# Token groups across sequences, chunk 0 on the hardware queues, three-chunk first MLP blocks, and stores issued by ScalarE

## Chip, cores and metric

The kernel runs on one core of one Trainium2 chip. The metric is device microseconds (us) by the run's timer. The trace of a run gives a *span*, from its first to its last instruction; on this kernel the timer reads about 1.8 us more than the span of the same run (219.26 against 217.5 for the trace of the kernel before).

Names: PE is TensorE, ACT is ScalarE, DVE is VectorE, POOL is GpSimd, SP is SyncE. A `q` behind a name (ACTq, SPq) marks the engine's sequencer issuing a transfer. Of the tiles, `q_hat` and `k_dec` are q and k multiplied by powers of the decay, and `qT` and `kT` are the transposed tiles.

## The reference, cut to what matters

```python
# q, k, v: (4 sequences, 8 heads, 768 tokens, 64); lam: one decay per head; blocks of 64 tokens
for b in range(nb):
    intra = (qb @ kb^T * Dmask) @ vb
    inter = (qb * lam_pow) @ kv_state
    out[:, :, sl] = intra + inter
    kv_state = lam_block * kv_state + (kb * rev_pow)^T @ vb      # serial along one sequence
x = out.transpose(0, 2, 1, 3).reshape(4 * 768, 512)
h = x @ w_in                                                      # 512 -> 2048
y = gelu_exact(h) @ w_out                                         # 2048 -> 512, float32 out
```

The kernels work in chunks of 128 tokens: 24 chunks, six in each sequence. The state is serial along a sequence and independent between sequences. Four chunks make a *group* of 512 tokens, and the MLP runs group by group, six groups in all. The attention of the next group is woven between the MLP's matmuls.

## The kernel before: the parts that matter here

A group is four successive chunks, whichever sequence they belong to (`b, so = n // 6, n % 6`). All casting loads are on POOL, all stores on SP.

```python
qkv_pool = tile_pool("qkv", bufs=8);  work_pool = tile_pool("work", bufs=3)
out_pool = tile_pool("outp", bufs=3)
# ... cut
nc.sync.dma_start(lam_b, lam[None, :].to_broadcast((128, H)))
nc.gpsimd.iota(pos, ...);  nc.gpsimd.iota(row, ...)
for item in "k0 q0 v0 k1 q1 k2 q2 v1 k3 q3 v2 v3".split():
    load(int(item[1]), item[0])                  # nc.gpsimd.dma_start, float32 -> bf16
# ... later: load_w_in(0), the first quarter of w_in, is POOL's 13th transfer

def dma_transposes(c):                           # chunks 8 to 23: transposed by the DMA engines
    nc.sync.dma_start_transpose(out=c.kT, in_=c.k...)
    nc.gpsimd.tensor_mul(q_hat, c.q, lam_p...)
    nc.sync.dma_start_transpose(out=c.qT, in_=q_hat...)

def mm2(io, part):                               # second MLP product of one chunk, in four parts
    # ... cut: four matmuls per part
    if part == NK2 // 4 - 1:
        o_sb = out_pool.tile([128, d_model], F32, tag="o_s", name="o_sb")
        nc.scalar.copy(o_sb, om[io])
        nc.sync.dma_start(out[r:r + C, :], o_sb) # the store
# ... cut: chunks 0 to 3 before the MLP; chunks 8 to 23 one by one, at set shares of a group
```

Of the kernel before, what the change touches and what calls it, by code (L numbers as in the profile page):

```python
# [8 lines left out]
F32 = mybir.dt.float32  # L9
# [6 lines left out]
def kernel(  # L16
# [23 lines left out]
    M = 4  # L40
    NG = NCH // M
    assert NG * M == NCH and M == 4 and NB == 6

# [4 lines left out]
    qkv_pool = ctx.enter_context(tc.tile_pool(name="qkv", bufs=8))  # L48
    work_pool = ctx.enter_context(tc.tile_pool(name="work", bufs=3))
# [9 lines left out]
    def chunk_of(name, n):  # L59
        b, so = n // NB, n % NB  # L60
        return dram[name][b, :, so * C:(so + 1) * C, :].rearrange("h si d -> si h d")
# [4 lines left out]


    lam_b = consts.tile([128, H], F32)
    nc.sync.dma_start(lam_b, lam[None, :].to_broadcast((128, H)))

    pos = consts.tile([128, 1], F32)
# [3 lines left out]

    for item in "k0 q0 v0 k1 q1 k2 q2 v1 k3 q3 v2 v3".split():
        load(int(item[1]), item[0])
# [14 lines left out]

    idle = consts.tile([128, 512], BF16)
# [4 lines left out]
    cmj = consts.tile([128, 1], F32)  # L98
    warm = consts.tile([128, 1], F32)
    nc.vector.tensor_scalar(ident, row, pos, None, op0=ALU.is_equal)  # L100
    nc.vector.tensor_scalar(cmask, row, pos, None, op0=ALU.is_ge)
    nc.vector.tensor_scalar(negj, pos, -1.0, None, op0=ALU.mult)
    nc.vector.tensor_scalar(cmj, pos, -1.0, float(C), op0=ALU.mult, op1=ALU.add)

    lam_blk = consts.tile([128, HP, 128], F32)
    first_blk = consts.tile([128, HP, 128], BF16)
    nc.vector.memset(lam_blk, 0.0)
    nc.vector.memset(first_blk, 0.0)
# [7 lines left out]
    lam_k = consts.tile([128, H], F32)  # L116
# [10 lines left out]
    nc.scalar.activation(lam_k, ln, ACT.Exp, scale=cmj)  # L127
    nc.scalar.activation(lam_c, ln_col, ACT.Exp, scale=float(C))
    nc.scalar.activation(lam_p, ln, ACT.Exp, scale=pos)
    lam_c_b = lam_c[:, :, None].to_broadcast((128, HP, D))  # L130

    def make_lam_blk():
        for hi in range(2):
            p = slice(hi * D, (hi + 1) * D)
            nc.vector.tensor_copy(lam_blk[p, :, p], lam_c_b[p])
# [10 lines left out]
    states = {}  # L146

    def bank(shape, dtype, tag, name):
        return ps.tile(shape, dtype, tag=tag, name=name, bufs=2 if tag in ("sc", "mh", "mo") else 1)

    def begin(n, early=False):
        c = Chunk()
        c.n, c.sb, c.early = n, n % NB, early
        c.q, c.k, c.v = (raw.pop((n, name)) for name in "qkv")
        return c

    def decay_k(c, eng):

        if c.sb == NB - 1:
            return  # L160
        c.k_dec = work_pool.tile([128, H, D], BF16, tag="kd", name="k_dec")
        if eng is nc.scalar:
            for h in range(H):
                nc.scalar.activation(c.k_dec[:, h, :], c.k[:, h, :], ACT.Copy, scale=lam_k[:, h:h + 1])
        else:
            scale = lam_k if c.early else lam_m
            eng.tensor_mul(c.k_dec, c.k, scale[:, :, None].to_broadcast((128, H, D)))  # L167

    def transposes(c, between=lambda: None):

        t_ps = [bank([128, HP, C], BF16, tag, "t_ps") for tag in ("mh", "mo" if c.early else "mh")]
# [7 lines left out]
        if c.n > 0:  # L179
            nc.scalar.copy(c.kT, t_ps[0])  # L180
        else:
            nc.vector.tensor_copy(c.kT, t_ps[0])
# [21 lines left out]
    def next_state(c):  # L204
        if c.sb == NB - 1:
            return
        if not c.early:
            return next_state_full(c)
        kv_ps = bank([128, HP, D], F32, "t", "kv_ps")
        for hp in range(HP):  # L210
            for hi in range(2):
                h = 2 * hp + hi
                nc.tensor.matmul(kv_ps[hi * D:(hi + 1) * D, hp, :], c.k_dec[:, h, :], c.v[:, h, :],
                                 start=True, stop=True)
        if c.n == M - 1:
            for hi in range(2):
                p = slice(hi * D, (hi + 1) * D)
                nc.vector.tensor_add(first_blk[p, :, p], kv_ps[p], states[c.n][1][p])
            states[c.n + 1] = first_blk, None
            return  # L220
        new = work_pool.tile([128, HP, D], BF16, tag="state", name="state")
        if c.sb == 0:
            nc.vector.tensor_copy(new, kv_ps)
        else:
            nc.vector.tensor_add(new, kv_ps, states[c.n][1])
        old = work_pool.tile([128, HP, D], F32, tag="old", name="old")
        states[c.n + 1] = new, old

    def decay_state(c):
        new, old = states[c.n + 1]  # L230
        for hp in range(HP):
            nc.scalar.activation(old[:, hp, :], new[:, hp, :], ACT.Copy, scale=lam_c[:, hp:hp + 1])

    def next_state_full(c):

        kv_ps = bank([128, HP, 128], F32, "t", "kv_ps")
# [3 lines left out]
        new = work_pool.tile([128, HP, 128], BF16, tag="state_f", name="state")  # L240
        if c.sb == 0:
            nc.vector.tensor_mul(new, kv_ps, lam_blk)
        else:
            tmp = work_pool.tile([128, HP, 128], F32, tag="tmp", name="tmp")
            nc.vector.tensor_add(tmp, kv_ps, states[c.n][0])  # L245
            nc.vector.tensor_mul(new, tmp, lam_blk)  # L246
        states[c.n + 1] = new, None

    def outputs(c, x_t, off, evacuate=True):
        o_ps = bank([128, HP, C], F32, "o", "o_ps")  # L250
        if c.sb > 0 and not c.early:
            for hp in range(HP):
                nc.tensor.matmul(o_ps[:, hp, :], states[c.n][0][:, hp, :], c.qT[:, hp, :],  # L253
                                 start=(hp == 0), stop=False, skip_group_check=True)
        elif c.sb > 0:
            for hp in range(HP):
                for hi in range(2):
                    p = slice(hi * D, (hi + 1) * D)
                    nc.tensor.matmul(o_ps[p, hp, :], states[c.n][0][p, hp, :], c.qT[p, hp, :],
                                     start=(hp == 0), stop=False, skip_group_check=True)  # L260
        for hp in range(HP):
            for hi in range(2):
                nc.tensor.matmul(o_ps[hi * D:(hi + 1) * D, hp, :], c.v[:, 2 * hp + hi, :], c.sc_m[:, hp, hi, :],  # L263
                                 start=(c.sb == 0 and hp == 0), stop=True, skip_group_check=True)
        c.x_o, c.o_ps = x_t[:, :, off * C:(off + 1) * C], o_ps
        if evacuate:
            empty_outputs(c)

    def empty_outputs(c):
        if c.n < 2 * M:  # L270
            nc.scalar.copy(c.x_o, c.o_ps)
        else:
            nc.vector.tensor_copy(c.x_o, c.o_ps)  # L273


    def mlp_blocks(g):
        T = M * C
        x_t = xT[g]
        g_t = g_pool.tile([128, NK2, T], BF16, tag="g", name="g_t")

        def mm1(kf):
            def run():
                h_ps = bank([128, T], F32, "mh", "h_ps")

                parts = [(0, T - C), (T - C, T)] if g == 0 and kf == 0 else [(0, T)]
                for lo, hi in parts:
                    for ki in range(NK1):
                        nc.tensor.matmul(h_ps[:, lo:hi], w_in_t[:, ki, kf * 128:(kf + 1) * 128], x_t[:, ki, lo:hi],  # L288
                                         start=(ki == 0 and lo == 0), stop=(ki == NK1 - 1), skip_group_check=True)
                nc.scalar.activation(g_t[:, kf, :], h_ps, ACT.Gelu)  # L290
            return run
# [3 lines left out]
        def mm2(io, part):  # L295
            def run():
                if part == 0:
                    om[io] = bank([128, d_model], F32, "mo", "o2_ps")
# [3 lines left out]
                if part == NK2 // 4 - 1:  # L302
                    o_sb = out_pool.tile([128, d_model], F32, tag="o_s", name="o_sb")
                    r = (g * M + io) * C
                    nc.scalar.copy(o_sb, om[io])  # L305
                    nc.sync.dma_start(out[r:r + C, :], o_sb)
            return run

        def mm2_half(io, half):

            def run():
                w = slice(half * (d_model // 2), (half + 1) * (d_model // 2))
                o2 = bank([128, d_model // 2], F32, "mo", "o2_ps")
# [4 lines left out]
                r = (g * M + io) * C  # L318
# [5 lines left out]
        blocks = [(mm1(kf), 4 * T) for kf in range(NK2)]  # L324
# [15 lines left out]
    next_load = [M]  # L340
# [6 lines left out]


    alloc_x(0)
    live = {}  # L350
    make_dmask()
    nc.scalar.activation(warm, pos, ACT.Gelu)

    idle_ps = {}

    def keep_warm(n, new=True):

        if new:
            idle_ps[0] = bank([128, 512], F32, "mo", "idle_ps")
        for _ in range(n):  # L360
            nc.tensor.matmul(idle_ps[0], idle[:, :128], idle, start=True, stop=True)  # L361

    def early(s, between=lambda: None):
        live[s] = begin(s, early=True)
        if s == 1:
            decay_k(live[s], nc.vector)
        transposes(live[s], between)
        if s != 1:
            decay_k(live[s], nc.scalar if s == 0 else nc.gpsimd)

    keep_warm(9)
    early(0, lambda: keep_warm(3, new=False))
    keep_warm(2, new=False)
    scores(live[0])
    keep_warm(2, new=False)
    early(1)
# [128 lines left out]
```

## Time and profile before

| | us |
|---|---|
| timer, median of 3 runs (lowest to highest) | 217.46 (217.44 to 217.77) |
| timer and span of the traced run | 219.26 and 217.5 |
| busy PE / ACT / POOL in the span | 204.9 / 91.1 / 105.8 |
| first MLP matmul | 19.37 |
| groups 0 to 4, from first matmul to first matmul of the next | 34.68, 35.12, 32.41, 32.19, 32.42 |
| group 5 with the tail | 31.31 |

### The profile page before, as it was taken

The numbers are of one execution on the slowest core, as the hardware profiler recorded it, in microseconds if no ns is written. First come the engines' busy times: TensorE is split into PE (matmuls) and PEld (weight loads), VectorE is DVE, ScalarE is ACT, GpSimd is POOL, SyncE is SP. The second block draws the span as 40 slices with busy tenths as digits, with TensorE's granted clock in tenths as the row PEclk, the third lists the DMA queues.
The fourth block names the chain that finished last, engine by engine and source line by source line (L and its number), as shares of the span: only waits on it lengthen the run. The fifth ranks groups of instructions, "written<-read, shape, count | busy, mean of one in ns | idle before, by whom it ended". The sixth has DMA issues, their size and how long they took to land.

```text
span 217.5 us, 3545 instructions
## 1 busy us (share of the span) xinstructions
PE 204.9 (94%) x1422; PEld 102.9 (47%) x1446; DVE 74.8 (34%) x120; ACT 91.1 (42%) x169; POOL 105.8 (49%) x120
## 2 busy tenths in 40 slices
PE   7679999999987999999999999999999999999993
PEld 2355444555443544444545444544445545444452
DVE  5884000478516243316225323315415323100000
ACT  6975772434563321365221375221465221566121
POOL 8998333998999999276950809113000000000000
PEclk9999999999999999999999999999999999999998
DMA  5999999999999999999999497515251012100112
GB/s 37 149 169 203 198 194 183 156 208 148 177 150 126 164 128 138 215 110 104 109 114 160 77 180 62 37 48 146 74 98 24 3 57 88 50 0 3 48 49 96
DMA packets 100272, 24.35 MB, mean 112 GB/s; under 512 B 92960, under 2 KB 97312, under 8 KB 100256
## 3 DMA queue, kind: packets, MB, share of 16 engines
q0 software_dynamic: 79104, 13.64, 84.4%
q1 hardware_dynamic: 21152, 10.50, 22.7%
q8 instruction: 11, 0.18, 0.3%
q14 instruction: 5, 0.04, 0.1%
HBM read 27.27 MB, written 6.29 MB: 154 GB/s over the span
## 4 chain that ended last, share of the span: by engine, by line
PE 73%; DMA 14%; POOL 9%; issue 2%; ACT 0%; POOLq 0%
PE o_ps L300 33%; PE h_ps L288 28%; DMA q_t<-in_q_dram 8%; DMA qT<-q_hat 3%; DMA w_in_t<-in_moe_w_in_dram 3%; PE o_ps L263 3%; PE sc_ps L198 3%; POOL k_t L65 3%; POOL q_t L65 2%; POOL v_t L65 2%; PE kv_ps L238 2%; PE o_ps L315 2%; PE o_ps L253 2%; POOL k_dec L167 1%; POOL q_hat L190 1%
## 5 line engine op out<-in xcount | busy, mean ns | idle before, releaser
L288 PE MATMUL h_ps<-x_t,w_in_t 128*128 128x512 bf16 (+2 forms) x378 | 84.8, 377 | 1.0 <-DMA w_in_t<-in_moe_w_in_dram 0.5
L300 PE MATMUL o_ps<-w_out_t,g_t 128*128 128x512 bf16 x355 | 81.8, 379 | 0.8 <-issue 0.3
L290 ACT ACTIVATE g_t<-h_ps 128x512 bf16<-128x512 f32 x96 | 57.3, 597 | 35.3 <-PE h_ps L288 35.3
L288 PEld LDWEIGHTS <-w_in_t 128*128 128x128 bf16 x388 | 37.3, 98 | 43.8 <-DMA w_in_t<-in_moe_w_in_dram 0.6
L300 PEld LDWEIGHTS <-g_t 128*128 128x128 bf16 x368 | 34.7, 98 | 39.6
L305 ACT COPY o_sb<-o_ps 128x512 f32<-128x512 f32 x23 | 13.5, 586 | 68.3 <-PE o_ps L300 62.5
L202 DVE TENSOR_TENSOR sc_m<-sc_ps,dmask 128x512 bf16<-128x512 f32 x48 | 30.8, 683 | 16.1 <-PE sc_ps L198 15.8
L273 DVE CAST x_t<-o_ps 128x512 bf16<-128x512 f32 x16 | 11.1, 692 | 71.4 <-PE o_ps L263 71.4
L190 POOL TENSOR_TENSOR q_hat<-q_t,lam_p 128x512 bf16<-128x512 bf16 x16 | 16.9, 1056 | 20.0 <-DMA qT<-q_hat 19.0
L167 POOL TENSOR_TENSOR k_dec<-k_t,lam_m 128x512 bf16<-128x512 bf16 x16 | 17.7, 1106 | 14.0 <-PE kv_ps L238 8.1
L65 POOL DMA_DIRECT2D k_t<-in_k_dram x24 | 22.1, 920 | 4.0 <-DMA w_out_t<-in_moe_w_out_dram 2.1
L65 POOL DMA_DIRECT2D q_t<-in_q_dram x24 | 21.5, 897 | 4.2 <-DMA w_out_t<-in_moe_w_out_dram 3.4
L65 POOL DMA_DIRECT2D v_t<-in_v_dram x24 | 21.4, 894 | 3.4 <-DMA w_out_t<-in_moe_w_out_dram 1.7
L198 PE MATMUL sc_ps<-qT,kT 64*128 64x128 bf16 x192 | 9.5, 218 | 3.8 <-DMA qT<-q_hat 2.6
L246 DVE TENSOR_TENSOR state<-tmp,lam_blk 128x512 bf16<-128x512 f32 x13 | 12.1, 932 | 0.5
L183 DVE TENSOR_TENSOR qT<-t_ps,lam_q 128x512 bf16<-128x512 bf16 x8 | 5.5, 689 | 18.9 <-PE t_ps L174 18.7
L263 PE MATMUL o_ps<-sc_m,v_t 128*64 128x128 bf16 x192 | 10.1, 225 | 0.0
L198 PEld LDWEIGHTS <-kT 64*128 64x128 bf16 x192 | 5.7, 94 | 8.3 <-issue 4.7
L361 PE MATMUL idle_ps<-idle 128*128 128x512 bf16 x21 | 7.5, 473 | 1.2 <-DVE idle L94 1.2
L245 DVE TENSOR_TENSOR tmp<-kv_ps,state 128x512 f32<-128x512 f32 x12 | 8.2, 681 | 0.0
L180 ACT COPY kT<-t_ps 128x512 bf16<-128x512 bf16 x7 | 4.1, 579 | 9.4 <-PE t_ps L174 9.4
L263 PEld LDWEIGHTS <-v_t 128*64 128x64 bf16 x192 | 6.2, 109 | 3.3 <-issue 0.8
(57 smaller groups left out, 82.7 us busy)
## 6 DMA issues: line engine op xcount, KB each, us to landing
out_dram<-o_sb SPq DMA_DIRECT2D x23, 256.0 KB, 2.6
k_t<-in_k_dram POOLq DMA_DIRECT2D x24, 128.0 KB, 4.6
q_t<-in_q_dram POOLq DMA_DIRECT2D x24, 128.0 KB, 5.9
v_t<-in_v_dram POOLq DMA_DIRECT2D x24, 128.0 KB, 5.9
w_in_t<-in_moe_w_in_dram POOLq DMA_DIRECT2D x4, 512.0 KB, 7.9
w_out_t<-in_moe_w_out_dram POOLq DMA_DIRECT2D x4, 512.0 KB, 15.1
kT<-k_t SPq DMA_TRANSPOSE x16, 4.7
qT<-q_hat SPq DMA_TRANSPOSE x16, 4.0
```

Source lines behind the costliest of these rows:

```text
L65: nc.gpsimd.dma_start(raw[n, name], chunk_of(name, n))
L167: eng.tensor_mul(c.k_dec, c.k, scale[:, :, None].to_broadcast((128, H, D)))
L190: nc.gpsimd.tensor_mul(q_hat, c.q, lam_p[:, :, None].to_broadcast((128, H, D)))
L198: nc.tensor.matmul(sc_ps[hi][:, hp, :], c.kT[p, hp, :], c.qT[p, hp, :], start=True, stop=True)
L202: nc.vector.tensor_mul(c.sc_m[:, :, hi, :], sc_ps[hi], dmask_r[:, :, hi, :])
L246: nc.vector.tensor_mul(new, tmp, lam_blk)
L263: nc.tensor.matmul(o_ps[hi * D:(hi + 1) * D, hp, :], c.v[:, 2 * hp + hi, :], c.sc_m[:, hp, hi, :], start=(c.sb == 0 and hp == 0), stop=Tru ...
L273: nc.vector.tensor_copy(c.x_o, c.o_ps)
L288: nc.tensor.matmul(h_ps[:, lo:hi], w_in_t[:, ki, kf * 128:(kf + 1) * 128], x_t[:, ki, lo:hi], start=(ki == 0 and lo == 0), stop=(ki == NK1 ...
L290: nc.scalar.activation(g_t[:, kf, :], h_ps, ACT.Gelu)
L300: nc.tensor.matmul(om[io], g_t[:, kf, io * C:(io + 1) * C], w_out_t[:, kf, :], start=(kf == 0), stop=(kf == NK2 - 1))
L305: nc.scalar.copy(o_sb, om[io])
```

## The change

The intent: start the MLP sooner, by taking chunk 0 off POOL's queue and letting the first MLP blocks run on three chunks; make the four chunks of a group independent (`b, so = n % 4, n // 4`), so that states and scores can be fed in pairs and asked for early; and free SP's queue for transposes, by letting ACT issue the stores.

```diff
-        b, so = n // NB, n % NB
+        b, so = n % B, n // B
-    qkv_pool = ... bufs=8        work_pool = ... bufs=3
+    qkv_pool = ... bufs=12       work_pool = ... bufs=6
     # outp keeps bufs=3
+    k_f = load_f32(0, "k", nc.scalar)
     nc.sync.dma_start(lam_b, lam[None, :].to_broadcast((128, H)))
+    q_f = load_f32(0, "q", nc.sync)
+    v_f = load_f32(0, "v", nc.sync)
+    load(1, "k")
     # ... the two iotas
-    for item in "k0 q0 v0 k1 q1 k2 q2 v1 k3 q3 v2 v3".split():
+    for item in "q1 k2 q2 v1 v2 k3 q3".split():
+    load_w_in(0)
+    load(3, "v")
     # ... cut
-            parts = [(0, T - C), (T - C, T)] if g == 0 and kf == 0 else [(0, T)]
+        split = g < 2            # first four blocks on three chunks, then one block for the fourth
     # ... cut
-                    nc.sync.dma_start(out[r:r + C, :], o_sb)
+                    nc.scalar.dma_start(out[r:r + C, :], o_sb)
     # ... cut
+    round_f32(0, "k", k_f, nc.vector.tensor_copy)
+    round_f32(0, "q", q_f, nc.vector.tensor_copy)
+    nc.scalar.copy(live[0].v, v_f)
+    # chunks 4 to 9 loaded, 8 and 9 requested; then k_dec of 4 to 7 on POOL
+    # groups 1 to 4: pair_a (two scores), pair_b (two inter, two kv, two intra), at set blocks
```

## The prediction

> **What bounds it now.** I read the page's busy table first, then the chain of waits, then the timeline in three stretches (start-up, group 0 to group 1, and the tail).
>
> ```profile
> PE 204.9 (94%) x1422; PEld 102.9 (47%) x1446; DVE 74.8 (34%) x120; ACT 91.1 (42%) x169; POOL 105.8 (49%) x120
> ...
> PE 73%; DMA 14%; POOL 9%; issue 2%; ACT 0%; POOLq 0%
> ```
>
> TensorE (PE) is the bound: nothing else passes 49%, and where the chain is not PE it is the start-up and the loads. So three things are worth time: when the dense MLP stream begins, how much PE work lies after that, and where PE stands still inside it. The timeline of the start-up answers the first:
>
> ```profile
> 11.99 0.84 POOL L87 DMA_DIRECT2D w_in_t<-in_moe_w_in_dram  x1
> ...
> 18.94 0.59 ACT L271 CAST x_t<-o_ps 128x512 bf16<-128x512 f32 x1 [1.50 <-PE o_ps L263]
> 19.37 0.88 PEld L288 LDWEIGHTS <-w_in_t 128*128 128x128 bf16 x8 [0.63 <-DMA w_in_t<-in_moe_w_in_dram]
> 19.37 1.05 PE L288 MATMUL h_ps<-x_t,w_in_t 128*128 128x384 bf16 x8 [0.47 <-DMA w_in_t<-in_moe_w_in_dram]
> ...
> 20.59 13.12 PE L288 MATMUL h_ps<-x_t,w_in_t 128*128 128x512 bf16 x59
> ```
>
> The MLP starts at 19.37 us, when the first quarter of w_in lands, 7.4 us after its issue at 11.99. The fourth chunk's x_t is ready at 19.53, so both limits stand together. From 20.59 to 33.55 lie 60 matmuls of 512 columns (one record is missing), so 0.216 us each. The PE timeline gives the cost of the attention's pieces, as differences of start times:
>
> ```profile
> 41.23 0.40 PE L198 MATMUL sc_ps<-qT,kT 64*128 64x128 bf16 x8
> 41.56 1.04 PE L300 MATMUL o_ps<-w_out_t,g_t 128*128 128x512 bf16 x4
> 42.44 0.39 PE L174 MATMUL t_ps<-ident,k_t 128*128 128x128 bf16 x4
> 42.66 0.39 PE L174 MATMUL t_ps<-ident,q_t 128*128 128x128 bf16 x4
> 42.88 0.39 PE L238 MATMUL kv_ps<-v_t,k_dec 128*128 128x128 bf16 x4
> 43.10 0.39 PE L253 MATMUL o_ps<-qT,first_blk 128*128 128x128 bf16 x4
> 43.42 0.41 PE L263 MATMUL o_ps<-sc_m,v_t 128*64 128x128 bf16 x8
> 43.77 1.04 PE L300 MATMUL o_ps<-w_out_t,g_t 128*128 128x512 bf16 x3
> ...
> 56.32 0.40 PE L198 MATMUL sc_ps<-qT,kT 64*128 64x128 bf16 x8 [0.38 <-DMA qT<-q_hat]
> ...
> 66.70 0.40 PE L198 MATMUL sc_ps<-qT,kT 64*128 64x128 bf16 x8 [2.18 <-DMA qT<-q_hat]
> ```
>
> Scores cost 0.33, transposes 0.44, the state (kv) 0.22, the inter part 0.32, the intra part 0.35. Inter takes as many matmuls as kv, so 0.10 of it is the turn to the narrower 128x64 tile of intra. The last two lines are the only large stalls of PE after the start: 0.4 and 2.2 us for a transposed q. The last matmul run ends at 214.06, and 3.4 us of copy, store and landing follow. So 217.5 = 19.4 + 194.7 + 3.4.
>
> [...]
>
> **The change part by part.**
>
> Start of the MLP. Before, w_in's first quarter is POOL's 13th transfer. After, three loads of chunk 0 leave POOL, the quarter is issued ahead of v of chunk 3, and one load goes ahead of the two iotas: eight loads then come first. POOL is free at about 0.85, so the issue starts at 0.85 + 0.44 (iotas) + 8 x 0.88 = 8.3, and with the same 7.4 us to landing it lands at 15.7. The attention must have three chunks by then. Its powers of lam still come from two 1.28 us table loads on ScalarE and end near 6.3 (same as before). From there VectorE is the chain: the mask 1.23 to about 6.9, qT of chunks 0 and 1 (2 x 0.69), the scores of 0 (1.29), qT of 2, scores of 1 and 2 (2 x 1.29): 12.9. Intra of chunk 2 and its 0.59 copy make three chunks ready near 14.2. So w_in decides, **15.7 us, a gain of 3.7**. Waiting for three chunks alone is worth little, since its limit comes earlier.
>
> Work moved behind the start. Inter: 20 chunks after, 17 before, + 3 x 0.22. kv: 20 against 17 (early chunks' states are put off into the stream), + 0.66. Intra of chunk 3 moves in, + 0.45. The split first blocks run the same columns[...], at most + 0.1, because before has a split block as well. Pairing keeps inter, kv and intra of two chunks together, so the tile turn is paid 13 times in place of 20: - 0.7. Sum **+ 1.2**.
>
> Stalls. Independent sequences let q of chunks 8 and 9 be asked for right behind the loads of chunk 9; I count qT of 9 landed at 57 to 58, and PE asking at 15.7 + 33.6 + 0.3 + 9.6 = 59.2 (group 0's work, a gap, ten blocks of group 1). So the 2.2 and 0.5 us vanish, **- 2.8** (the 0.54 is 0.38 and what goes with it). But GpSimd now has four k_dec (1.05 each) in a row, then six loads, two q_hat and two k_dec: about 11 us before the states of 8 and 9 are fed, against about 66 us on PE. That fits to within a microsecond either way. I take **+ 0.7** back for this and for the tight bank rotation of chunks 4 to 7.
>
> Stores on ScalarE. 22 issues of 0.6 us are 13 us on an engine busy 91 of 217 us, beside PE; a gelu takes 0.60 against 0.86 us of matmuls. It frees the sync queue, whose transposes waited behind stores (two stores took from 77.98 to 81.77), but PE didn't wait there. I give it 0; the last stores stay on the sync queue, so the tail stays 3.4.
>
> Sum: 217.5 - 3.7 + 1.2 - 2.8 + 0.7 = 212.9.
>
> **Rivals.** (1) The DMA engines, not POOL, pace the start. For: counting packet records in the trace, 1,160 to 1,210 packets of 128 bytes end in each microsecond from 6 to 14, and a tensor is 1,024 of them, so engines take 0.85 us a tensor, no faster than POOL issues. Three float32 tensors beside them have the same packet count, twice the written bytes. Against: the hardware queue begins about 1.4 us sooner (first packet of lam at 1.74, of k at 3.14). If written bytes count, w_in lands at 17 to 18 and the time is 214.5 to 215.5. (2) VectorE or the lam chain becomes the bound: [...]any delay there shifts the whole chain. The slack is 1.5 us, so only a delay past that costs; 213 to 214.5. (3) A new wait in group 1: k_dec behind a long GpSimd list, or a late qT of chunk 11; PE would stand 1 to 3 us at a kv or scores, 213.5 to 215.5. (4) It goes better: [...]w_in lands near 14.5, nothing stalls: 211.
>
> **Range and chances.** The middle is 212.9, a trifle under the 2% line of 213.1. Rivals 1 to 3 can each add 1 to 2 us and are partly exclusive; rival 4 and smaller stalls take 1 to 2 off. I put 8 in 10 on 210.6 to 215.2. Faster by over 2% gets 0.55: a schedule with positions set by hand per group looks tuned, so late arrivals of 1 us have probably been moved away. Within 2% gets 0.43, slower 0.02, since nothing I found adds more than the start gains.
>
> **What would show it.** Right: first MLP matmul near 15.7, released by w_in; no wait on qT over 0.5 us near 60; group 0 about 34 us and group 1 about 34.5 us long; each later group near 32.3; ScalarE's busy time still under half. Wrong: MLP starting past 17; the chunk-0 loads landing later than 6 us; PE waiting for k_dec, qT or a bank in group 0 or 1; gelus late because of a store's issue.

What the trace of the kernel before shows: a casting load of q, k or v took POOL 0.88 to 0.96 us, the first one 1.06; matmuls of 128 columns start 56 ns apart and those of 512 columns 216 (medians), so four of the short take as long as one of the long to within 0.01 us. The 0.6 us for a store's issue is half of a merged row of two stores (41.08, 1.20 us, with the pause between them); by its own record an issue of SP took 0.33 us at the median. And the 0.10 us that the prediction puts down to the tile turn is seen in the kernel after with whatever stands ahead of intra: there, at 101.97, eight matmuls of inter take 0.45 us and the eight of kv behind them, before intra, 0.54.

## More of the kernel before

All comparisons are between runs of the fast state, unless a run is named as slow or its state as unknown.

The prediction shows the lines that bound the kernel. Two more views are needed later. The first is the page's slices of the span: each digit is a fortieth of it, in tenths of busy time, or of full clock.

```profile
PE   7679999999987999999999999999999999999993
PEclk9999999999999999999999999999999999999998
```

PE is busy from the fourth slice to the last but for two slices that are a little lower, and its clock is full all the way (0.997 as the mean of the span). The second view is the timeline of two engines at the end of group 0 (start, duration, engine, line, operation, and in brackets the idle time before it and what ended it): first SP's queue, then ACT.

```profile
53.58 1.66 SPq L306 DMA_DIRECT2D out_dram<-o_sb  x2
55.34 1.23 SPq L189 DMA_TRANSPOSE kT<-k_t  x1
```

```profile
52.49 0.59 ACT L305 COPY o_sb<-o_ps 128x512 f32<-128x512 f32 x1 [0.71 <-PE o_ps L300]
54.30 0.59 ACT L305 COPY o_sb<-o_ps 128x512 f32<-128x512 f32 x1 [0.42 <-PE o_ps L300]
```

ACT copies a result out of PSUM as soon as PE has it, and goes on. The store and whatever it has to wait for are SP's business.

## The result, and the profile after

After: 220.44 us, median of 4 runs (219.67 to 220.9). Before: 217.45 (217.26 to 217.77, 4 runs). The ratio is 1.0132, 95% interval 1.0101 to 1.0164; it is within the 2% that counts as the same, on the slow side, and outside the predicted range. Ratios in this document are the mean time of one kernel's fast runs over that of the other's fast runs of the same rounds, so they are not quite the quotient of the medians quoted.

The page of the kernel after: PE's slices, its clock, and the chain of waits by engine.

```profile
PE   7599999999499999979999999999999999999994
PEclk9769999999979999999999999999999999999999
...
PE 69%; DMA 22%; POOL 3%; issue 3%; ACT 1%; ACTq 0%; POOLq 0%
```

The busy total of PE is the same as before (204.8 us). New are a hole in the eleventh slice (the 4) and a dent in the eighteenth (the 7), a clock that is low in the second, third and twelfth slice, and more DMA in the chain (22% for 14%). The first matmul of each group in the PE timeline, with the differences taken, says where it lies. The third row is a single run. The rows below the second belong to experiments told later; they are here because the table is read as one.

| us | MLP start | group 0 | 1 | 2 | 3 | 4 | 5 and tail | span |
|---|---|---|---|---|---|---|---|---|
| before, as traced first | 19.37 | 34.68 | 35.12 | 32.41 | 32.19 | 32.42 | 31.31 | 217.5 |
| **after** | 18.02 | 34.55 | **38.54** | **33.65** | 32.08 | 31.19 | 31.07 | 219.1 |
| before, traced again | 19.73 | 35.37 | 32.88 | 32.42 | 32.19 | 32.42 | 31.29 | 216.3 |
| stores on SP, 3 buffers | 17.82 | 34.55 | 38.48 | 32.08 | 32.08 | 31.19 | 31.00 | 217.2 |
| stores on SP, 6 buffers | 17.88 | 34.55 | 34.69 | 32.08 | 32.08 | 31.18 | 31.04 | 213.5 |
| stores on ACT, 6 buffers | 18.59 | 34.55 | 38.56 | 33.21 | 32.08 | 31.19 | 31.12 | 219.3 |
| the fastest version | 16.67 | 34.56 | 33.70 | 32.08 | 32.08 | 31.19 | 31.12 | 211.4 |

Groups 3 and 4 run as intended. Three places do not: the start is 2.3 us behind the prediction, group 1 some 4.8 longer than it can be (last row), group 2 some 1.6.

**Group 1.** The ACT timeline of the kernel after, and from PE's timeline the row that stood still:

```profile
52.35 0.58 ACT L289 COPY o_sb<-o_ps 128x512 f32<-128x512 f32 x1
57.25 0.34 ACTq L290 DMA_DIRECT2D out_dram<-o_sb  x1
57.64 0.87 ACT L274 ACTIVATE g_t<-h_ps 128x384 bf16<-128x384 f32 x2 [4.71 <-DMA qT<-q_hat]
58.39 0.59 ACT L243 CAST x_t<-o_ps 128x512 bf16<-128x512 f32 x1
```

```profile
59.04 1.40 PE L272 MATMUL h_ps<-x_t,w_in_t 128*128 128x128 bf16 x16 [3.02 <-ACT x_t L243]
```

The copy of group 0's last result ends at 52.93. Its store is issued at 57.25, and in the 4.3 us between ACT does nothing at all, though two gelus and the copy of the group's fourth chunk are due. The bracket blames the gelu's wait on `qT<-q_hat`, a transpose that a gelu has no use for: all 173 operations of ACT (copies, activations and issues) start in this trace in the order of the program, and it was the *store* ahead of the gelu that waited. The store's own row shows 0.34 us and no wait: it begins at 57.25, and the wait has a record of its own, at 57.20, which the views leave out. So the wait of a store must be read from the idle time of the next ordinary instruction on its engine.

Why should a store wait for a transpose of another chunk? The program's wait list, the waits that each instruction carries in the compiled program, tells. It is no view of the trace: it is read from the program after building it. The transfers issued by SP and ACT take turns on eight completion semaphores (counters that tell when a transfer has landed), DMAHW0 to DMAHW7, both engines together, in one order that is fixed in the compiled program. The records of the trace, behind the views, name the semaphore of each transfer: all 61 of SP and ACT have one of eight numbers, 107, 109, 110, 113 and 115 to 118. In this program a transfer that takes a semaphore waits for the transfer that had it last, eight places before, unless its engine has waited for that one already. The list of the kernel after, from its start, in that order:

```
ACT  load k_f                          DMAHW0
SP   loads lam_b, q_f, v_f             DMAHW1 to 3
SP   transposes kT, qT of chunk 8      DMAHW4, 5
SP   transposes kT, qT of chunk 9      DMAHW6, 7
ACT  store 1 of group 0                DMAHW0       waits for k_f
ACT  store 2                           DMAHW1
ACT  store 3                           DMAHW2       waits for q_f
SP   transposes of chunks 10 and 11    DMAHW3 to 6
ACT  store 4 of group 0                DMAHW7       waits for qT of chunk 9
```

SP issued qT of chunk 9 at 54.58, and the store went out when it had landed. The trace bears the list out: its records give both transfers the same semaphore, 118. The transpose's landing counts it up to the full at 57.17, ACT's wait on it has its record at 57.20, and the store's issue stands at 57.25. The prediction had that landing right ("57 to 58"), and saw that PE doesn't need it before 59; it did not see that a store needs it.

The price of the shared semaphores is here a wait of 4.3 us between transfers that have no data in common. In the kernel before these waits stood on SP (its records have them ahead of the stores at 77.98 and 81.44, for instance, on semaphores 116 and 117), which does nothing but issue transfers. Now they stand on the engine that PE needs.

The clock adds to it. The windows view, in steps of 2 us (stretch, length, busy PE, PEld, DVE, ACT, POOL with instruction counts, then PEclk, mean DMA share, GB/s), gives for the kernel after

```profile
60.00:62.00 2.00, 1.78 (x15) 1.45 (x14) 1.06 (x2) 0.60 (x1) 2.00 (x3) 0.50 1.64 105
```

and 0.90 and 0.75 in the windows beside it: 2 x (0.10 + 0.50 + 0.25) = 1.7 us of full clock lost, as an estimate, after a stop of 3.02. The granted clock was 0.50 for 3.41 us, from 59.59 to 63.00. A stop of 2.18 us in the kernel before left it at 1.00, and one of 2.06 us in a run told below was followed by half the clock, so the length of the stop alone doesn't decide it. Stop and clock are 4.7 of the 4.8 us.

**Group 2** has the same thing again, smaller. All engines' timeline of the kernel after:

```profile
94.52 0.34 ACTq L290 DMA_DIRECT2D out_dram<-o_sb  x1
94.95 0.58 ACT L289 COPY o_sb<-o_ps 128x512 f32<-128x512 f32 x1 [6.51 <-PE sc_ps L206]
95.59 1.02 PE L272 MATMUL h_ps<-x_t,w_in_t 128*128 128x512 bf16 x4 [1.18 <-ACT o_sb L289]
...
96.15 2.06 ACT L274 ACTIVATE g_t<-h_ps 128x512 bf16<-128x512 f32 x4 [0.61 <-DMA qT<-q_hat]
```

The store of a result that was copied at 87.85 is issued at 94.52. By the wait list the third and fourth store of group 1 wait for kT and qT of chunk 15, which SP issued at 91.94 and 93.26; they landed at 94.44 and 95.69, and the two stores were issued at 94.52 and 95.77. The copy behind it is late, so a PSUM bank is late, and PE stands 1.2 us; with 0.2 more at 96.80 that is the 1.4 to 1.6 us that the group is too long.

**The start.** POOL and PE in the kernel after:

```profile
9.43 0.76 POOL L100 DMA_DIRECT2D w_in_t<-in_moe_w_in_dram  x1 [0.61 <-DMA k_t<-in_k_dram]
```

```profile
9.19 0.61 PE L185 MATMUL t_ps<-ident,k_t 128*128 128x128 bf16 x4 [0.90 <-DMA k_t<-in_k_dram]
...
10.10 0.61 PE L185 MATMUL t_ps<-ident,q_t 128*128 128x128 bf16 x4 [0.29 <-DMA q_t<-in_q_dram]
...
18.02 1.46 PE L272 MATMUL h_ps<-x_t,w_in_t 128*128 128x384 bf16 x8
```

The MLP starts 0.05 us after the third chunk's copy ends on ACT (17.97), so it is the attention that comes last; the first quarter of w_in had landed at 17.22, 0.8 us before. Chunk 0's three loads took 5.0, 5.8 and 6.9 us from issue to landing, and POOL's first load, k of chunk 1, issued at 1.25, landed only at about 9.1: in the packet records its first packet ends after 5 us, and from 2 to 7 us 142 to 1,075 packets end in each microsecond, most of them the float32 loads' of 256 bytes; before, from 6 us on, it was 1,129 to 1,208 of 128 bytes (the prediction says 1,160 to 1,210). PE was busy for 2.21 of the 5 us from 5 to 10, and its granted clock was 0.50 from 8.38 to 15.21. What took the clock down is not shown. The windows view:

```profile
5.00:10.00 5.00, 2.21 (x16) 0.96 (x15) 3.12 (x5) 3.00 (x8) 4.39 (x6) 0.84 2.01 184
10.00:15.00 5.00, 4.43 (x39) 2.67 (x40) 3.45 (x6) 3.09 (x7) 4.26 (x7) 0.50 2.25 166
```

The slow clock is a part of the lateness. The run *Group 0 waits for four chunks*, told below, has the same loads in the same order, and its k of chunk 1 landed at 8.94. But there PE was at full clock from 9.6 us on, in the kernel after only from 15.2:

```profile
9.89 0.40 PE L185 MATMUL t_ps<-ident,q_t 128*128 128x128 bf16 x4 [0.30 <-DMA q_t<-in_q_dram]
```

The same four transposes took 0.40 us for 0.61, and the third chunk was ready at 16.59, 1.4 us sooner than at 17.97, of which the loads explain 0.2. At that clock w_in, at 17.05, would have been the last link.

The quarter of w_in was issued at 9.43, 1.1 us after the predicted 8.3. Here, too, there is a rotation of eight semaphores, POOL's own (99 to 106 in the records): the quarter is POOL's ninth transfer and waits on 99, which its first has, the k of chunk 1 that came late, counted up to the full at 9.15.

### The profile page after: what moved, and what is told of

Same layout as the page of the kernel before. It is cut to its first block, busy times and chain, and to the rows that moved or that the text cites. A ratio compares the mean times of both kernels' runs of the same rounds, so it can differ in the third digit from the quotient of the medians.

```text
span 219.1 us, 3495 instructions
## 1 busy us (share of the span) xinstructions
PE 204.8 (93%) x1417; PEld 105.3 (48%) x1442; DVE 77.3 (35%) x124; ACT 86.4 (39%) x152; POOL 100.9 (46%) x115
## 4 chain that ended last, share of the span: by engine, by line
PE 69%; DMA 22%; POOL 3%; issue 3%; ACT 1%; ACTq 0%; POOLq 0%
PE h_ps L272 30%; PE o_ps L284 30%; DMA q_t<-in_q_dram 11%; DMA w_in_t<-in_moe_w_in_dram 5%; DMA k_t<-in_k_dram 4%; DMA qT<-q_hat 2%; PE o_ps L239 2%; PE kv_ps L218 2%; PE sc_ps L206 2%; PE o_ps L233 2%; PE o_ps L299 2%; POOL v_t L66 1%; POOL k_t L66 1%; ACT g_t L274 1%; POOL q_hat L198 1%
## 5 line engine op out<-in xcount | busy, mean ns | idle before, releaser
L272 PE MATMUL h_ps<-x_t,w_in_t 128*128 128x512 bf16 (+2 forms) x404 | 87.2, 366 | 5.2 <-ACT x_t L243 3.0
L274 ACT ACTIVATE g_t<-h_ps 128x512 bf16<-128x512 f32 (+1 forms) x98 | 57.0, 590 | 40.6 <-PE h_ps L272 34.7
L272 PEld LDWEIGHTS <-w_in_t 128*128 128x128 bf16 x416 | 39.0, 99 | 46.9 <-issue 6.1
L198 POOL TENSOR_TENSOR q_hat<-q_t,lam_p 128x512 bf16<-128x512 bf16 x16 | 17.8, 1112 | 26.6 <-DMA q_t<-in_q_dram 12.4
L225 DVE TENSOR_TENSOR tmp<-kv_ps,state 128x512 f32<-128x512 f32 x16 | 11.0, 687 | 36.4 <-PE kv_ps L218 36.4
L66 POOL DMA_DIRECT2D q_t<-in_q_dram x23 | 20.7, 901 | 6.6 <-DMA w_out_t<-in_moe_w_out_dram 3.3
L66 POOL DMA_DIRECT2D k_t<-in_k_dram x23 | 21.1, 919 | 4.4 <-DMA w_out_t<-in_moe_w_out_dram 1.6
L178 POOL TENSOR_TENSOR k_dec<-k_t,lam_m 128x512 bf16<-128x512 bf16 x16 | 16.3, 1041 | 0.0
L239 PE MATMUL o_ps<-sc_m,v_t 128*64 128x128 bf16 x192 | 8.6, 227 | 0.5 <-DVE qT L191 0.5
L206 PE MATMUL sc_ps<-qT,kT 64*128 64x128 bf16 x192 | 8.6, 226 | 0.2 <-DVE qT L191 0.2
```

The source lines that it names most:

```text
L66: nc.gpsimd.dma_start(raw[n, name], chunk_of(name, n))
L178: eng.tensor_mul(c.k_dec, c.k, lam_m[:, :, None].to_broadcast((128, H, D)))
L198: nc.gpsimd.tensor_mul(q_hat, c.q, lam_p[:, :, None].to_broadcast((128, H, D)))
L206: nc.tensor.matmul(sc_ps[hi][:, hp, :], c.kT[p, hp, :], c.qT[p, hp, :], start=True, stop=True)
L225: nc.vector.tensor_add(tmp, kv_ps, states[c.b])
L239: nc.tensor.matmul(c.o_ps[hi * D:(hi + 1) * D, hp, :], c.v[:, 2 * hp + hi, :], c.sc_m[:, hp, hi, :], start=(c.so == 0 and hp == 0), stop=T ...
```

## The experiments

All ten kernels computed the right result. Two theories of the loss in group 1 stood against each other: **the store waits on ACT for an unrelated transfer** (semaphore theory), or **three output buffers are too few** for stores that land late, whoever issues them (buffer theory). The first three runs and a later one make a table of two by two.

| ratio to before (median us) | 3 buffers | 6 buffers |
|---|---|---|
| stores on ACT | 1.0132 (220.44), the change itself | 1.0155 (221.48) |
| stores on SP | 1.0028 (219.08) | 0.9855 (215.30) |

**Stores back on SP, three buffers.**

```diff
-                    nc.scalar.dma_start(out[r:r + C, :], o_sb)
+                    nc.sync.dma_start(out[r:r + C, :], o_sb)
```

> The changed kernel with its 23 full stores back on the sync queue, nothing else. Lane theory (a store on ScalarE stands behind the completion of the hardware transfer eight before it, the transposed q of chunk 9, and holds ScalarE's whole queue): ScalarE no longer waits inside a store. But the sync queue now keeps the four stores of group 0 behind the four transposes of chunks 8 and 9, and there are three store buffers, so the fourth copy out of PSUM must wait for the first store, about 58 us: the stall in group 1 then comes back as a buffer wait of the same size, 219 to 221 us. Rival (ScalarE is simply late with its own work around chunk 7, issue cost of stores included): 13 us of issue less on ScalarE, stall shrinks, 216 to 218 us. Third reading (the stall is the store's wait alone and buffers do not matter): 214.5 us.

Measured: 219.08 us (218.87 to 219.33), ratio 1.0028 (0.9963 to 1.0093). (At the 0.34 us that an issue took on ACT, 23 stores are 7.8 us, not the 13 of the rival.) The stall of group 2 is gone (32.08 us), that of group 1 is not. SP's queue, ACT and PE in their timelines:

```profile
54.79 3.33 SPq L290 DMA_DIRECT2D out_dram<-o_sb  x4
```

```profile
57.17 0.58 ACT L289 COPY o_sb<-o_ps 128x512 f32<-128x512 f32 x1 [5.41 <-DMA out_dram<-o_sb]
```

```profile
57.81 0.83 PE L272 MATMUL h_ps<-x_t,w_in_t 128*128 128x384 bf16 x4 [2.64 <-ACT o_sb L289]
```

On SP the stores of group 0 stand behind the transposes of chunks 8 and 9 (the last of them issued at 53.40), and go out as a pack of four at 54.79. The fourth *copy* now waits for a buffer, and ACT with it. So the buffer limit is real, but only once SP holds the stores; the same 4 us come by another road.

**Stores on SP and six buffers.** As above, and

```diff
-    out_pool = ctx.enter_context(tc.tile_pool(name="outp", bufs=3))
+    out_pool = ctx.enter_context(tc.tile_pool(name="outp", bufs=6))
```

> As e1_sync_stores, with six store buffers in place of three. Lane theory: nothing on ScalarE waits for a transposed tile any more, neither by lane nor by buffer; group 1 falls from 38.9 to about 34.5 us and group 2 from 33.7 to 32.4, so 220.4 - 4.4 - 1.3 = 214.7 us, range 214.0 to 215.5. Rival (ScalarE late by its own work): within 1 us of e1_sync_stores.

Measured: 215.30 us (214.87 to 215.79), ratio 0.9855 (0.979 to 0.9921); as expected, though whether it is under or over 2% is not certain. ACT at the same place:

```profile
52.20 0.58 ACT L289 COPY o_sb<-o_ps 128x512 f32<-128x512 f32 x1 [0.38 <-PE o_ps L284]
53.29 0.49 ACT L274 ACTIVATE g_t<-h_ps 128x384 bf16<-128x384 f32 x1 [0.50 <-PE h_ps L272]
```

The gelu follows the copy by 0.5 us and waits for nothing but PE. This is the change with its stores on SP and with three buffers more: faster than before by 1.5%.

**Stores on ACT and six buffers.** The missing corner: the change with the line for six buffers alone.

> The changed kernel, stores on ScalarE as it has them, with six store buffers in place of three and nothing else. Lane theory: buffers are not what ScalarE waits for; the fourth store still stands behind the transposed q of chunk 9, so 220.4 us as the changed kernel, 219.7 to 221. Rival (the gain of e1b_sync_stores_6buf over e1_sync_stores came from buffers alone): about 215.5.

Measured: 221.48 us in three fast runs (221.04 to 221.55), 224.88 in a slow one; ratio 1.0155 (1.0073 to 1.0237); no gain. Its ACT timeline shows the same wait for the same transfer:

```profile
57.84 0.34 ACTq L290 DMA_DIRECT2D out_dram<-o_sb  x1
58.23 0.87 ACT L274 ACTIVATE g_t<-h_ps 128x384 bf16<-128x384 f32 x2 [4.72 <-DMA qT<-q_hat]
```

So the buffer theory falls for the change itself: with the stores on ACT, buffers do nothing.

**One more transfer ahead.** If it is the turn on eight semaphores, then a single small transfer put in front of group 0's first store moves every later one by one place, and the fourth store no longer meets qT of chunk 9.

```diff
+                    if g == 0 and io == 0:
+                        nc.scalar.dma_start(lam_d, lam[None, :].to_broadcast((128, H)))
                     nc.scalar.dma_start(out[r:r + C, :], o_sb)
```

> The changed kernel, stores still on ScalarE, with one more 4 KB load issued on ScalarE just ahead of the first store. It shifts the lanes so that the fourth store of group 0 reuses the lane of that small load and no longer that of the transposed q of chunk 9; the stores of group 1 still reuse lanes of the transposes of chunk 13. Lane theory: the 3 us stall near 59 us goes, with the slow clock after it, the one near 94 us stays: 220.4 - 4.4 = 216.0 us, range 215.3 to 217.0. Rival (store issue on ScalarE, [...]or ScalarE's load): unchanged or 0.4 us slower, 220 to 221.

Measured: 220.46 and 221.58 us in two fast runs, 224.33 and 226.26 in two slow ones; ratio of the fast ones 1.0116 (1.0011 to 1.0222). The expected time was missed. The trace, of a slow run (224.33, clock 0.985), shows both halves of the answer. ACT's timeline:

```profile
52.76 0.34 ACTq L293 DMA_DIRECT2D out_dram<-o_sb  x1
...
98.31 2.06 ACT L275 ACTIVATE g_t<-h_ps 128x512 bf16<-128x512 f32 x4 [2.39 <-DMA qT<-q_hat]
```

and PE's waits (waiter, what it waited for, us in total, times, longest):

```profile
PE kv_ps L219 <- POOL k_dec L179: 2.8, 2, 2.2
```

The fourth store goes out at 52.76, straight behind its copy, by the wait list waiting for the small transfer and no longer for qT of chunk 9. Adding 4 KB of work to the queue took the first stall away, which no theory of load or buffers expects. But the time didn't follow. Group 1 is still 38.18 us long: PE, earlier now, stood 2.8 us for k_dec, and the clock fell behind that stop (1.7 us by the windows, worked out as above). And group 2 is 37.69 us long: the stores at 94.89 and 97.92 still wait for kT and qT of chunk 15, which SP issued at 92.33 and 94.75, later than in the change (91.94 and 93.26), and PE stood 2.1 and 2.0 us behind them, with 1.7 us of clock lost again. So the mechanism of the first stall is confirmed and my sum for the run was wrong: what was gained at 57 was given back at 70 and 96. How much of that a fast run has is open, as the trace is of a slow one. POOL makes k_dec behind the q_hat of chunk 11, which waited 4.04 us for its load of q here, and 1.57 in the run with stores on SP and six buffers; why that load was slower is open.

**The kernel before with its stores on ACT.** Same one-line edit, in the other direction, in the kernel before.

> The kernel before with its full stores on ScalarE, nothing else. Lane theory: stores of groups 0 and 1 then wait on lanes of transposes too, but those had mostly landed when the store is due, so only one or two of them hold ScalarE for 1 to 3 us: 217.5 to 220. Rival (stores on ScalarE cost their issue time only): 217.3 to 217.7 with no store waiting for a transposed tile. If the sync queue's blocked transposes were what stalled chunk 9 in the kernel before: 215.

Measured: 218.57 us (218.09 to 219.0), ratio 1.0004 (0.9936 to 1.0071). No gelu waits for a transpose; PE's list of waits has one line of the kind:

```profile
PE o_ps L300 <- ACT o_sb L305: 1.6, 1, 1.6
```

This wait is not of that kind either: ACT's first store, at 40.77, took 3.71 us to issue where the others' median is 0.34, and what held it is not shown. By the wait list no store of group 0 waits for a transpose here: the fourth follows the second store on its semaphore. So stores on ACT don't bring the stall by themselves. They cost what the transfer eight places ahead happens to be late, and in the kernel before, whose chunks are asked for one by one, that was nothing that the trace shows. Stores on ACT alone change nothing (1.0004), the rest of the change alone gains (0.9855 with six buffers), and the two together lose (1.0132, 1.0155). Which part of the rest makes the late transfer, the asking for transposes in pairs most likely, was not taken apart further.

**The kernel before, traced again.** The same program, one run of unknown state.

> The kernel before unchanged, for a profile of its usual execution: the trace on record is of an execution of 219.3 us by the timer, and the runs lie near 217.4 and near 219.5. If the 2.2 us stall for the transposed q of chunk 9 is what the slower ones have, an execution near 217.4 has a span of 215.6 and no such stall, and the prediction counted on a gain that the usual runs don't hold. If the stall is there in a fast run too, the gain was real and was lost elsewhere.

Measured: 218.07 us, span 216.3. PE's waits for a transposed q, first in the trace on which the prediction was built, then in this one:

```profile
PE sc_ps L198 <- DMA qT<-q_hat: 2.6, 2, 2.2
```

```profile
PE sc_ps L198 <- DMA qT<-q_hat: 0.4, 1, 0.4
```

Group 1 is 32.88 us long here, and 35.12 in the first trace. SP issued the transpose that is waited for at 60.09 here and at 59.67 there, and it landed at 65.23 and 66.57. The kernel before has quicker and slower runs: in the rounds of the first experiments 217.22, 217.38, 217.59 and 218.74, 219.32, 219.67 (twice). The first trace is of the slower kind. That the 2.2 us wait makes the two kinds is likely from these two traces, and not shown for the untraced runs.

**The start, three variants.** All three are the version with stores on SP and six buffers (start 17.88), with one thing changed, so that no store stall lies over them. They ran in other rounds and on another chip than that version, and the last time before the MLP that PE came to its full clock was 14.1 us there, and 4.3, 9.6 and 10.1 in the three variants. So what each is worth is better read from when the transfers landed than from the start of the MLP or from medians that lie 1 us apart.

*Chunk 0 through POOL's casts again.*

```diff
-    k_f = load_f32(0, "k", nc.scalar);  q_f, v_f = ... nc.sync;  load(1, "k")
-    for item in "q1 k2 q2 v1 v2 k3 q3".split():
+    for item in "k0 q0 v0 k1 q1 k2 q2 v1 v2 k3 q3".split():
-    # the two rounding copies on VectorE and the one on ScalarE
```

> Based on e1b_sync_stores_6buf (215.3 us, MLP starting at 17.9). Chunk 0 is loaded by POOL as casts again, ahead of chunk 1; no float32 copies. Theory D (the DMA engines pace the start and the float32 loads only take their turn there, so POOL's freed slots are worth little): 11 loads then stand before w_in in place of 8 + 3, one fewer than in the kernel before, so the MLP starts at 19.4 - 0.9 = 18.5 us, and the time is 0.3 to 1.0 us longer than e1b. Theory P of the prediction (POOL's issue slots pace it): three more slots of 0.88 us, start at 20.5, time 2.6 us longer.

Measured: 216.68 us (216.41 to 217.38), ratio 0.9954 (0.9914 to 0.9993). PE at the start of the MLP:

```profile
18.60 2.74 PE L267 MATMUL h_ps<-x_t,w_in_t 128*128 128x384 bf16 x8 [2.06 <-DMA w_in_t<-in_moe_w_in_dram]
```

The MLP starts only 0.7 us later than with the hardware queues, and now w_in decides: it landed at 18.55, and the third chunk was ready at 16.55. Three casting loads more on POOL, 2.6 us of its time, bring w_in 1.4 us later (17.19 in the base, where the attention came last). After the wait of 2.06 us the eight matmuls took 2.74 us in place of 1.46, at half the clock (granted 0.80 as the mean of 15 to 20 us).

*Group 0 waits for four chunks.*

```diff
-        split = g < 2
+        split = g == 1
+    keep_warm(4);  outputs(live[3])      # ahead of the MLP; group 0's visits one block sooner
```

> Based on e1b_sync_stores_6buf. Group 0's first MLP blocks wait for all four chunks as in a plain group; chunk 3's output stands before them. The three-chunk start is worth the time until chunk 3's output, about 19.9 + 0.6 us against 17.9, less the 0.35 us of PE work that moves out of the stream: MLP starts at 20.2, time 1.5 to 2.3 us longer. Rival (w_in's landing, not the chunks, sets the start, so splitting is worth nothing): start before 18.6, time within 0.5 us.

Measured: 216.30 us (215.88 to 217.04), ratio 0.9943 (0.9896 to 0.9989); start at 19.04, after a 0.68 us wait for the fourth chunk's copy. Against the base this is 1.2 us at the start and about 1.0 in the time, less than the 1.5 to 2.3 expected. But with this trace's clock three chunks could have started when w_in landed, at 17.05: as an estimate the split is worth 2.0 us at the start when the clock is the same.

*Only v of chunk 0 through POOL.*

```diff
-    v_f = load_f32(0, "v", nc.sync)
-    for item in "q1 k2 q2 v1 v2 k3 q3".split():
+    for item in "q1 v0 k2 q2 v1 v2 k3 q3".split():
-    nc.scalar.copy(live[0].v, v_f)
```

> Based on e1b_sync_stores_6buf. Only k and q of chunk 0 come as float32 over the hardware queues; v of chunk 0 is cast by POOL after q of chunk 1. Theory S (the hardware loads, at under 1,000 packets a microsecond, hold back POOL's first transfers, so k of chunk 1 lands at 9 us and the attention of chunks 0 to 2 is late): k of chunk 1 lands 1.3 us sooner, MLP starts at about 17.0, time 0.5 to 1.0 us shorter. Rival (POOL's first transfers are late whatever the hardware queues carry): no change of k of chunk 1, w_in one slot later, 0.5 to 0.9 us longer.

Measured: 215.58 us (215.05 to 216.26), ratio 0.99 (0.9855 to 0.9945). PE at the start, and its longest sum of waits:

```profile
16.64 1.47 PE L271 MATMUL h_ps<-x_t,w_in_t 128*128 128x384 bf16 x8 [0.47 <-DMA w_in_t<-in_moe_w_in_dram]
```

```profile
PE kv_ps L217 <- POOL k_dec L177: 1.4, 3, 0.6
```

One float32 load of 256 KB less on the hardware queues brings k of chunk 1 from 9.09 to 7.63 and the first quarter of w_in from 17.19 to 16.60, although POOL has one load more. The third chunk comes at 16.19 for 17.82 and the MLP's start at 16.64 for 17.88, but this is the load and the clock together: here, too, PE is at full clock from 10.1 us on (the windows view says 1.00 before that, but the clock's records only begin there, and four transposes still take 0.61 to 0.63 us), and with that clock and all three loads the third chunk was ready at 16.59 in the variant above. So of the 1.6 us some 0.4 can be the load's. The time doesn't follow: group 1 is 0.9 us longer, since PE now comes to the state updates before POOL has made k_dec; POOL makes it behind a q_hat that waits for its load of q (1.50 us for chunk 11, 3.55 for chunk 13).

**The same, with k_dec of chunks 8 to 19 on VectorE.**

```diff
         for m in (n - 2, n - 1):
-            decay_k(live[m], nc.gpsimd)
+            decay_k(live[m], nc.vector)
```

> Based on e7_v0_pool (215.6 us; MLP at 16.6, but three waits of PE for a k_dec from POOL, 1.4 us together). The k_dec of the pairs from chunk 8 on are made by VectorE in place of POOL. If those waits are what took back the earlier start (new-wait theory): none of them is left and the time is 214.2 us, range 213.7 to 214.8. Rival (the earlier start is taken back by the DMA supply, which is the same): another wait, for a transposed q or a load, takes their place and the time stays at 215.3 to 215.8.

Measured: **213.36 us** (213.06 to 213.99, 6 runs), against 217.98 (216.9 to 219.77, 8 fast runs; three more were slow) for the kernel before in the same rounds: ratio 0.9786 (0.9742 to 0.983). This beats both kernels; that it is by over 2% is not certain, as the interval reaches to 0.983. The trace's view of the tile k_dec (durations least, median and most in ns):

```profile
L177 DVE TENSOR_TENSOR k_dec<-k_t,lam_m x16: 677/683/1528, 17.7 to 132.5; 128x512 bf16<-128x512 bf16 x16
```

VectorE takes 0.68 us where POOL takes 1.05, and no state update waits any more. Group 1 falls from 35.62 to 33.70 us, by 1.9, of which the waits were 1.4; the rest I didn't trace further.

## Why the prediction was wrong, step by step

| step, in us | predicted | measured |
|---|---|---|
| MLP start | 15.7 | 18.02 |
| start to end of the span, stores apart | 197.2 (194.7 + 1.2 - 2.8 + 0.7 + 3.4) | 194.7 (201.1 less the 6.4 below) |
| stores on ACT, groups 1 and 2 | 0 | 6.4 |
| span | 212.9 | 219.1 |
| timer over span | 0 | 1.8 |

The 6.4 is worked out from the table of groups: (38.54 + 33.65) of the change less (33.70 + 32.08) of the version in which nothing waits. The two edits together agree: stores on SP with six buffers take 5.6 us off the span (219.1 to 213.5). Stores on SP alone take off 1.9 (217.2), because the three buffers then hold ACT up in group 1; the prediction looked at the buffers as little as at the waits.

**The step that failed: "Stores on ScalarE ... I give it 0".** The prediction weighed ACT's busy time, 13 us of issues beside PE, and found room. It asked what an issue *costs* and not what an issue *waits for*. The issue itself is cheaper than it said (0.34 us, not 0.6; SP's issues in the trace of before took 0.33 at the median). The wait is 4.3 us at group 0's fourth store, and at group 1's third it is 6.1 us from the end of its copy (88.44) to its issue (94.52). It had "gelus late because of a store's issue" among its signs of being wrong, and this was the sign that came; but it could have been read beforehand, as the program could be built and its wait list lay open.

**The start, a size that was off.** Rival 1, the transfers pacing the start with w_in at 17 to 18, named the right cause and nearly the right figure, but w_in was not the last link. Both limits were too early: w_in, predicted for 15.7, came in the variant with v on POOL at 16.64, and in the change at 17.22 (issued at 9.43, 7.8 us to landing, where the prediction kept 7.4); the third chunk, predicted for 14.2, was ready at 17.97. The prediction took POOL's loads to run as they did before and the hardware queues' loads to come on top of it free of charge. The variant with v moved shows that they aren't: one load less there, k of chunk 1 1.5 us and w_in 0.6 us sooner. And it counted no half clock at the start, where PE before was at full clock from 4.5 us on; as far as two single traces show it, this is the other reason why the third chunk came after w_in. A cost of the rounding copies on VectorE isn't seen: POOL's loads beside them took 0.89 and 0.92 us each.

**The stalls, - 2.8.** Right for the trace that was read, wrong for the usual run: the second trace of before has 0.4 us of such waits. Most of this gain isn't there in such a run.

**Span against timer.** The sum began with the span, 217.5, and ended in a number that was compared with the timer's 217.46; that they were alike is chance, as that trace's run took 219.26 by the timer. In the same units the prediction was about 212.9 + 1.8 = 214.7, which is 1.3% under the median of before. With that the odds of faster by over 2% would not have been 0.55.

**What held.** Work after the start: the prediction took 1.2 us more PE work and gave 0.7 back for k_dec and banks. The fastest version needs 194.7 us from start to end of span; the trace of before needed 198.1, less 2.8 of stalls 195.3. So neither the 1.2 nor the 0.7 is seen in the end, because the new order saved more than the 0.7 that was counted for it. Against before, group 2 of the change has one inter more, group 3 one inter and one kv more, and group 4 three kv fewer, as its chunks end their sequences. At 0.22 us each, and with groups that are 0.33, 0.11 and 1.23 us shorter, that leaves some 0.55 us saved in each of the three, as an estimate; that it is all the tile turn isn't shown. Rival 3, k_dec late in group 1, is in the version with stores on SP and six buffers (0.6 us), and in the one with the earlier start (1.4 us). Rival 2 came in part: lam landed at 4.37 us for 3.29 before, the last of its powers that VectorE needs was ready at 7.38 for 6.3, which the prediction had kept, and VectorE came to the mask at 7.33, behind the rounding of q of chunk 0, which had just landed. But the next link waited for k and q of chunk 1, at 9.15 and 10.05, so this delay didn't set the start. Rival 4 did not come.

## What to carry to other kernels

Before moving a transfer's issue to another engine, read in the program's wait list what that issue waits for, not only what it costs: here ACT stood still for 4.3 us, as a store waited for a transpose eight transfers ahead with which it shares no data. When a wait is named that the waiting instruction can't need, look for the instruction ahead of it on the same engine. And take the base of a sum in the unit in which the result is timed, from more than one trace.
